# Attention features and experts on one core: projections moved ahead, scatters spread over two tiles, and the norm's root given to ScalarE with one exact step on VectorE

## The chip, the core and the metric

The kernel runs on one core of one Trainium2 chip. The metric is the device time in microseconds of one execution, lower is better. Times shown beside each other come from executions of the same kernel; the traces come from one profiled execution each.

## The reference

Two layers in a row: attention by positive random features, without softmax, and a mixture of eight experts of which each token takes one. Cut to what is computed:

```python
# batch 8, heads 8, seq 576, head_dim 64, 128 features
def phi(x):                       # x = q or k, scaled by 64 ** -0.25
    h = x @ omega.T - sum(x * x) / 2
    return exp(h - max(h)) / sqrt(128)
kv  = einsum('bhsm,bhsd->bhmd', phi(k), v)
z   = phi(k).sum(over s)
att = (phi(q) @ kv) / (phi(q) @ z + 1e-6)
x = att as (4608 tokens, 512)
xn = x / (norm(x) + 1e-6);  en = expert_emb / (norm(expert_emb) + 1e-6)
logits = xn @ en.T / tau
e = argmax(logits);  gate = softmax(logits)[e]
out = gate * (relu(x @ w1[e]) @ w2[e])     # 512 -> 1024 -> 512
```

The queries are drawn larger than the keys. Everything is in float32.

## The kernel before

**Attention** (to about 240 us, its end to 300). 36 tiles of 128 tokens. Iteration `i` of the loop at the end of the first part projects keys of tile `i` and queries of tile `i - 6` (`proj`), each in two halves `a` of four heads, and pairs them: first key half 0 with query half 1, then key half 1 with query half 0. `feats` takes the negative maximum of each head on VectorE (`nm`) and exponentiates on ScalarE (`ft`). `kvmm` adds the keys of tile `i - 1` to the key sums, `qtr` transposes query features (`tr`), `qcopy` copies them out (`qp`), `num` makes the numerators, denominators and logits of a tile (`nu`), and `evacuated` divides them into a row `xr` on VectorE. The order on TensorE and GpSimd, and in the loop on VectorE and ScalarE, is that of the code. Two pairs of PSUM banks, `px` and `py`, hold the projections; the transposes use `px`, the pair of the first projections.

Every third tile, `routed` chooses the expert of three tiles and each token's row in a list sorted by expert, in steps that the lists `spare`, `mid` and `ends` place at points of this and the next iteration; its last step issues three scatters on GpSimd's queue (one per tile) that write the rows `xr` to memory. When the first expert is known, the first two blocks of its tokens are computed between the last attention iterations (`first_steps`).

**Experts** (from about 301 us). 38 steps `t`, each for 128 rows of one expert, the first two within the attention. A step multiplies its rows by `w1` and, two steps behind, hidden rows by `w2`. Each float32 factor is split into a high and a low part, and three products are summed, so a step has 24 + 24 matmuls (`pa` and `nu`). Its other work in the loop, all in the order of the code on every engine:

- VectorE: the low part of the hidden rows (`hl`, L900), the gated result (`scaled`, L247), the high parts of the next weights (`w1h`, `w2h`, L205); then half of the 16-bit planes of the step's products and of the next rows (`pl`, L862), half of the transposed planes put together again (`wd`, L880), and the low part of the rows (`xl`, L899), with which the next step's third matmul begins.
- ScalarE: the other half of the planes (L861) and of the reassembly (L882), the high parts `xh` and `hh` (L894, L896), and the sums of squares of the rows (`sq`, L253).
- GpSimd: the low parts of the weights (`w1l`, `w2l`, L206), and between them the scattered store of a finished block (L272).
- SyncE: transposes of the planes (L868), rows, weights.

The gate needs the norm of each row. It is found for batches of three steps: in steps `t` that 3 divides (and in `SHIFT - 1`), `norms_of` runs on VectorE after the casts and ahead of the first `pl`. It calls `root`, a shift and a subtraction on the bits and three Newton steps, twelve instructions on 128 x 3 numbers (L120 to L131), and two more (L256, L257). `exps_of` then exponentiates the logits with that norm on ScalarE at the end of the step, and in the step after, `inverted` (L265, L266) stands on VectorE at the same place, ahead of `pl`.

Lines of this text are those of the kernel before.

Of the kernel before, what the change touches and what calls it, by code (L numbers as in the profile page):

```python
# [22 lines left out]
P = 128  # L23
# [30 lines left out]
def attention_moe(ctx: ExitStack, tc: tile.TileContext, qT, kT, v1, omT, emb, tau, w1q, w2q, xs, out):  # L54
# [51 lines left out]
    put, got, outs, last_x, junks = [], [], [], [], []  # L106
    W = {"w1": (w1q, w1h, w1l), "w2": (w2q, w2h, w2l)}

    padrow = w1l[:, 1, 2, 0:PAY].bitcast(F32)
    nc.gpsimd.memset(padrow, 0.0)  # L110
    nc.gpsimd.memset(padrow[:, PAY - 1 : PAY], BIGID)
# [135 lines left out]
        nc.vector.tensor_scalar(xg[:, 0:DM], po, gate, None, op0=ALU.mult)  # L247


    def squares(xg, n2):  # L250
        junk = gp.tile([P, DM], BF16, name=f"sq_{len(junks)}", tag="sq", bufs=1)
        junks.append(junk)
        nc.scalar.activation(junk, xg[:, 0:DM], AF.Square, accum_out=n2)  # L253
# [10 lines left out]
    def inverted(total):  # L264
        nc.vector.tensor_scalar(total, total, 1e-9, None, op0=ALU.add)  # L265
        nc.vector.reciprocal(total, total)  # L266
# [13 lines left out]
    with ExitStack() as c1:  # L280
# [104 lines left out]
            )  # L385

        def qtr(i, a):
            st["tr", i, a] = tr = ps.tile([P, 512], F32, name=f"tr{i}_{a}", tag="px", bufs=2)
            for h in range(4):
                nc.tensor.transpose(tr[:, h * P : (h + 1) * P], st["fq", i, a][:, h, :], ident)  # L390

# [21 lines left out]

        def num_out(i):
            g, gi = divmod(i, G)
            st["xr", i] = xr = p1.tile([P, PAY], F32, name=f"xr{i}", tag="xr", bufs=5)
            nc.gpsimd.tensor_copy(xr[:, PAY - 1 :].bitcast(I32), ids[:, i : i + 1])
            if gi == 0:
                st["lg", g] = small.tile([P, G, H, E], F32, name=f"lg{g}", tag="lg", bufs=2)
            rr = small.tile([P, 2, 4], F32, name=f"rr{i}", tag="rr", bufs=3)  # L420
            nc.vector.tensor_scalar(rr, pn[:, :, :, D], EPS, None, op0=ALU.add)
# [14 lines left out]
        def routed(g):  # L436
# [76 lines left out]
        def first_steps():  # L513


            new = lambda n, tag: ps.tile([P, 512], F32, name=f"fs_{n}", tag=tag, bufs=2 if tag == "py" else 1)
# [22 lines left out]
            for t in range(NPRE):  # L539
                hs[t] = rawp.tile([P, F], F32, name=f"hp{t}", tag="raw_w1")  # L540
                turned(xgp[t], 0, new(f"x{t}", f"kv{t}"), *pre_x[t])
                squares(xgp[t], n2[:, t : t + 1])
# [13 lines left out]
            yield from up(1, 1, range(4), new("a11", "py"))  # L556
# [3 lines left out]
            yield from turn(1, 1, "py")  # L560
            yield from down(0, range(4, 8), po)
            yield from down(1, range(8), new("o1", "kv1"))

# [59 lines left out]
        for i in range(NTILE + LAG + 1):  # L623
# [3 lines left out]
            loadq(iq + 2)  # L627
            ks, qs = i < NTILE, 0 <= iq < NTILE
            if ks and qs:
                pairs = [("k", i, 0, "px"), ("q", iq, 1, "px")], [("k", i, 1, "py"), ("q", iq, 0, "py")]  # L630
            elif ks:
                pairs = [("k", i, a, "px") for a in range(2)], []
            else:
                pairs = [("q", iq, a, "py") for a in (1, 0)] if qs else [], []
            filling = i > NTILE
            proj(*pairs[0])
            if later is not None:
                evacuated(later)
            for p in pairs[0][: 1 if i < LAG else 2]:
# [8 lines left out]
            if filling:  # L648
                filled(1 if i <= NTILE + 2 else 2)
            go(spare, i)  # L650
            proj(*pairs[1])
            if later is not None and later % G == G - 1 and later < NTILE - 1:
                steps = routed(later // G)

                for d, key in ((mid, i), (ends, i), (spare, i + 1), (mid, i + 1), (ends, i + 1)):
                    at(d, key).append((next, steps, None))
            go(mid, i)
            if not qs and iq >= 2:
# [213 lines left out]
    with tc.manual_schedule(engines={ET.PE, ET.Activation, ET.DVE, ET.Pool, ET.SP}):  # L872
# [28 lines left out]
            yield  # L901


        n2s, nrms, totals, gates = {}, {}, {}, {}
        batch = lambda t: divmod(t - NPRE, 3)

        def squares_of(*steps):
            for v in steps:
                b, j = batch(v)
                if j == 0:  # L910
                    n2s[b] = few("n2", f"b{b}", 3)
                squares(xg[v], n2s[b][:, j : j + 1])
# [23 lines left out]
        for t in range(NPRE, NSTAT):  # L936
# [36 lines left out]
            computed("w1", t, products(pa[0], xt[t], "w1", par, low, 0, True, True))  # L973
            if t == NPRE or NPRE + 1 < t < XPE - 1:
                xt[t + 1] = x_turned(t + 1, xg[t + 1])
            if t % 3 == 0 and t > SHIFT or t == SHIFT - 1:
                norms_of(batch(t)[0])
            elif t % 3 == 1 and t > SHIFT:
                inverted(totals[batch(t)[0]])
            elif t == SHIFT:  # L980
                inverted(totals[0])
            if near:
                h = words(t)
                nc.scalar.activation(h[:, 0:512], pa[0], AF.Relu)
# [16 lines left out]
            if late and not early:  # L1001
                rejoin(t - 1, wn[0], 0, F, 1)
            if t == SHIFT:
                ended()
            if NPRE + 1 < t < SHIFT:
                split("w2", u)
# [26 lines left out]
            if t % 3 == 0 and t > SHIFT or t == SHIFT - 1:  # L1033
                exps_of(batch(t)[0])
            if t + 3 < NSTAT:
                xg[t + 3] = x_of(t + 3, reg("row", t + 3))
        weights("w2", ends)
        hid[ends] = h_turned(ends, h)
        for u in (ends - 1, ends):
# [10 lines left out]
    with tc.If(tot > NSTAT):  # L1050
        with tc.For_i(NSTAT, tot, 1) as i:
# [9 lines left out]
            squares(xgl, n2)  # L1061
            nrm = root(gp, n2, 1, "x")
            norms(nrm)
            exps(xgl, nrm, total)
# [55 lines left out]
```

## Time and profile before

| | us |
|---|---|
| time, median of 3 runs | 784.7 (780.26 to 785.14) |
| time of the profiled execution | 788.04 |
| its span, first to last instruction | 786.5 |
| attention loop, 35.0 to 240.9 | 205.9 |
| end of attention, tables, 240.9 to 301.3 | 60.4 |
| expert steps 2 to 8, 301.3 to 382.7 | 81.4 |
| expert steps 9 to 36, 382.7 to 743.8 | 361.1 |
| last step and end, 743.8 to 786.5 | 42.7 |

Busy time over the span: TensorE 696.0, VectorE 597.1, ScalarE 382.5, GpSimd 299.1 us. In the profile PE is TensorE's matmuls and PEld its weight loads, DVE is VectorE, ACT ScalarE, POOL GpSimd and SP SyncE. A row of the timeline gives start, duration, engine, line, operation, what is written and read, and in brackets the idle time before it and what ended that. `L120` is a line of the kernel.

The waits and the timeline are read here more than the busy shares: TensorE is busy 88% of the span, and this figure does not tell the rate at which its matmuls run. The clock granted to TensorE is 0.956 on average over the span.

### The profile page before, as it was taken

The numbers are of one execution on the slowest core, as the hardware profiler recorded it, in microseconds if no ns is written. First come the engines' busy times: TensorE is split into PE (matmuls) and PEld (weight loads), VectorE is DVE, ScalarE is ACT, GpSimd is POOL, SyncE is SP. The second block draws the span as 40 slices with busy tenths as digits, with TensorE's granted clock in tenths as the row PEclk, the third lists the DMA queues.
The fourth block names the chain that finished last, engine by engine and source line by source line (L and its number), as shares of the span: only waits on it lengthen the run. The fifth ranks groups of instructions, "written<-read, shape, count | busy, mean of one in ns | idle before, by whom it ended". The sixth has DMA issues, their size and how long they took to land. (4 is left out here: it accounts for less than half of the span.)

```text
span 786.5 us, 17992 instructions
## 1 busy us (share of the span) xinstructions
PE 696.0 (88%) x5977; PEld 570.2 (73%) x5978; DVE 597.1 (76%) x1109; ACT 382.5 (49%) x1038; POOL 299.1 (38%) x296
## 2 busy tenths in 40 slices
PE   6899999998997987998889897989898998989884
PEld 5778878877876775776668685868676776777663
DVE  2368767778876562789798988898889889898951
ACT  4487767767876511732534343434343443434320
POOL 2000111111754232544536363636353544354442
PEclk9999999999999999999999899989999999899988
DMA  5354544548742127845958585867776686858530
GB/s 193 88 157 124 178 156 158 166 150 269 257 166 83 56 78 260 265 125 171 241 132 231 147 215 133 230 149 205 153 211 168 194 196 168 200 163 192 149 94 37
DMA packets 142376, 131.85 MB, mean 168 GB/s; under 512 B 106758, under 2 KB 106886, under 8 KB 142288
## 3 DMA queue, kind: packets, MB, share of 16 engines
q1 hardware_dynamic: 135968, 110.30, 52.1%
q0 software_dynamic: 6320, 20.38, 6.8%
q8 instruction: 55, 0.90, 0.5%
q14 instruction: 33, 0.27, 0.1%
HBM read 83.78 MB, written 21.97 MB: 134 GB/s over the span
## 5 line engine op out<-in xcount | busy, mean ns | idle before, releaser
L206 POOL TENSOR_TENSOR w1l<-raww,w1h 128x1024 f32 x34 | 89.4, 2631 | 218.3 <-DVE w1h L205 213.8
L240 PE MATMUL pa<-w1h,xl 128*128 (+1 forms) x280 | 118.8, 424 | 38.6 <-DVE xl L899 38.6
L240 PE MATMUL nu<-w2h,hh 128*128 (+1 forms) x288 | 113.2, 393 | 6.0 <-DVE xg L247 3.4
L240 PE MATMUL pa<-w1h,xh 128*128 (+1 forms) x280 | 116.5, 416 | 0.5 <-POOL w1l L206 0.2
L240 PE MATMUL pa<-w1l,xh 128*128 (+1 forms) x280 | 115.7, 413 | 0.0
L240 PE MATMUL nu<-w2h,hl 128*128 (+1 forms) x288 | 113.1, 393 | 0.2 <-DVE hl L900 0.2
L240 PE MATMUL nu<-w2l,hh 128*128 (+1 forms) x288 | 112.6, 391 | 0.0
L330 ACT ACTIVATE ftk<-pjk,nmk 128x128 f32<-128x128 f32 x288 | 82.5, 384 | 55.4 <-DVE nmk L327 51.3
L896 ACT ACTIVATE hh<-wd 128x1024 fp32r<-128x1024 f32 x34 | 36.0, 1060 | 130.7 <-DVE wd L880 130.7
L240 PEld LDWEIGHTS pa<-w1h,xl 128*128 128x128 f32 x280 | 56.8, 203 | 58.0 <-DVE xl L899 45.7
L321 PE MATMUL pjk<-om,kt 64*128 64x128 f32 x576 | 88.2, 308 | 9.9 <-DMA kt<-kT 5.3
L330 ACT ACTIVATE ftq<-pjq,nmq 128x128 f32<-128x128 f32 x288 | 84.1, 409 | 13.5 <-DVE nmq L327 13.1
L861 ACT ACTIVATE pl<-pa 128x512 uint16<-128x512 uint16 x68 | 39.5, 586 | 103.3 <-DMA t<-pl 86.5
L206 POOL TENSOR_TENSOR w2l<-raww,w2h 128x1024 f32 x34 | 82.1, 2414 | 8.9 <-DVE w2h L205 8.2
L321 PE MATMUL pjq<-om,qt 64*128 64x128 f32 x576 | 81.2, 294 | 3.2 <-DVE qp L398 1.4
L321 PEld LDWEIGHTS pjk<-om,kt 64*128 64x128 f32 x576 | 71.2, 204 | 16.2 <-issue 7.1
L327 DVE TENSOR_REDUCE nmk<-pjk 128x4 f32<-128x512 f32 x72 | 48.9, 686 | 36.6 <-PE pjk L321 20.0
L321 PEld LDWEIGHTS pjq<-om,qt 64*128 64x128 f32 x576 | 66.8, 194 | 7.7 <-issue 3.8
L472 POOL DMA_INDIRECT xs<-xr,posi x36 | 35.9, 996 | 86.6 <-DVE lg L423 33.7
L240 PEld LDWEIGHTS nu<-w2h,hh 128*128 128x128 f32 x288 | 54.5, 189 | 18.5 <-issue 7.4
L240 PEld LDWEIGHTS pa<-w1h,xh 128*128 128x128 f32 x280 | 57.1, 204 | 13.4 <-POOL w1l L206 0.7
L240 PEld LDWEIGHTS pa<-w1l,xh 128*128 128x128 f32 x280 | 56.6, 202 | 12.8
(297 smaller groups left out, 1363.9 us busy)
## 6 DMA issues: line engine op xcount, KB each, us to landing
raww<-w1q SPq DMA_DIRECT2D x38, 512.0 KB
raww<-w2q SPq DMA_DIRECT2D x38, 512.0 KB
kt<-kT SPq DMA_DIRECT2D x36, 256.0 KB
qt<-qT SPq DMA_DIRECT2D x36, 256.0 KB
xgp<-xs SPq DMA_DIRECT2D x20, 260.5 KB
xg<-xs SPq DMA_DIRECT2D x18, 260.5 KB
rf<-w1q SPq DMA_DIRECT2D x4, 512.0 KB
rf<-w2q SPq DMA_DIRECT2D x4, 512.0 KB
```

Of the source, the lines that this page charges most:

```text
L206: il = nc.gpsimd.tensor_tensor(at(l, dp), raw, at(h, dp).bitcast(F32), op=ALU.subtract)
L240: done.append(nc.tensor.matmul(dst, x[:, c * P : (c + 1) * P], ws.rearrange("p o f -> p (o f)"), start=(begin and i == 0 and k == 0), stop ...
L321: nc.tensor.matmul(st["pj" + w, i, a][:, c, :], st[w, i][r, c, :], om[r, :], start=True, stop=True)
L327: nc.vector.tensor_reduce(nm, pj, axis=AX.X, op=ALU.max, negate=True)
L330: nc.scalar.activation(ft[:, h, :], pj[:, h, :], AF.Exp, bias=nm[:, h : h + 1])
L472: w = nc.gpsimd.indirect_dma_start(out=xs, out_offset=bass.IndirectOffsetOnAxis(ap=posi[:, j : j + 1], axis=0), in_=xr, in_offset=None, bo ...
L861: nc.scalar.activation(planes[1][:, o : o + 512], halved(src)[:, :, 1], AF.Copy)
L896: nc.scalar.activation(hh, wd[:, 0:F], AF.Relu)
```

## The change

Four things change together.

1. **Attention.** Both pairs of projections are issued at the start of an iteration; the key sums, the transposes and the numerators follow. The banks change roles: the first pair and the transposes use `py`, the second pair `px`. Where only keys are projected, iterations alternate between the two pairs of banks; where only queries are, they use `px`. `first_steps` swaps its banks likewise.
2. **Scatters.** `routed` yields before each scatter, so that the three go out at three points of two iterations. There are six buffers `xr` instead of five, and one `lg` instead of two.
3. **The root.** ScalarE takes `Sqrt` of three sums of squares at the start of a step that 3 divides (and of step 4). In the step after, `norms_of` and `exps_of` stand ahead of `scaled`: VectorE forms (n2 / rough + rough) / 2 + 1e-6 and its inverse in five instructions. In the step after that, `inverted` stands at the same place.
4. **Squares.** The unused output of the squares goes to a buffer of the second part, or of the hidden rows in `first_steps`, and not to a pool that lives throughout.

```diff
         def qtr(i, a):
-            st["tr", i, a] = tr = ps.tile([P, 512], F32, name=f"tr{i}_{a}", tag="px", bufs=2)
+            st["tr", i, a] = tr = ps.tile([P, 512], F32, name=f"tr{i}_{a}", tag="py", bufs=2)
...
             for j in range(G):
+                yield
                 xr = st["xr", g * G + j]
                 w = nc.gpsimd.indirect_dma_start(
...
-                pairs = [("k", i, 0, "px"), ("q", iq, 1, "px")], [("k", i, 1, "py"), ("q", iq, 0, "py")]
+                pairs = [("k", i, 0, "py"), ("q", iq, 1, "py")], [("k", i, 1, "px"), ("q", iq, 0, "px")]
             elif ks:
-                pairs = [("k", i, a, "px") for a in range(2)], []
+                pairs = [("k", i, a, ("px", "py")[i % 2]) for a in range(2)], []
             else:
-                pairs = [("q", iq, a, "py") for a in (1, 0)] if qs else [], []
+                pairs = [("q", iq, a, "px") for a in (1, 0)] if qs else [], []
             filling = i > NTILE
             proj(*pairs[0])
+            proj(*pairs[1])
...
             go(spare, i)
-            proj(*pairs[1])
...
+        def roots_of(b):
+            rough[b] = few("rough", f"b{b}", 3)
+            nc.scalar.activation(rough[b], n2s[b], AF.Sqrt, bias=tiny)
 
         def norms_of(b):
-            nrms[b] = root(gp, n2s[b], 3, f"b{b}")
-            norms(nrms[b])
+            nrms[b] = few("nrm", f"b{b}", 3)
+            nc.vector.reciprocal(nrms[b], rough[b])
+            nc.vector.tensor_tensor(nrms[b], nrms[b], n2s[b], op=ALU.mult)
+            nc.vector.tensor_tensor(nrms[b], nrms[b], rough[b], op=ALU.add)
+            nc.vector.tensor_scalar(nrms[b], nrms[b], 0.5, 1e-6, op0=ALU.mult, op1=ALU.add)
+            nc.vector.reciprocal(nrms[b], nrms[b])
...
+            if t == SHIFT - 1 or t > SHIFT and t % 3 == 0:
+                roots_of(batch(t)[0])
+            elif t == SHIFT or t > SHIFT and t % 3 == 1:
+                norms_of(batch(t)[0] if t > SHIFT else 0)
+                exps_of(batch(t)[0] if t > SHIFT else 0)
+            elif t > SHIFT:
+                inverted(totals[batch(t)[0] - 1])
             if t > SHIFT:
                 for v in po:
                     scaled(po[v], xg[v], gates[v])
...
-            if t % 3 == 0 and t > SHIFT or t == SHIFT - 1:
-                norms_of(batch(t)[0])
-            elif t % 3 == 1 and t > SHIFT:
-                inverted(totals[batch(t)[0]])
```

Three places show the moves. In the lists below, a row has the line, the operation, what it writes and reads, and its width; equal neighbours are counted. Numbers in names are those of the tiles.

TensorE in attention iteration 9, before: the end of the first projections, the key sums of tile 8, and the start of the second projections.

```order
L321 MATMUL pjk_0_733<-om,kt_534 128x128
L321 MATMUL pjq_1_734<-om,qt_538 128x128
L345 MATMUL kva_1_0_431<-vt8v,ftk_0_645 64x65 x8
L345 MATMUL kva_1_1_440<-vt8v,ftk_1_697 64x65 x8
L321 MATMUL pjk_1_784<-om,kt_534 128x128
L321 MATMUL pjq_0_785<-om,qt_538 128x128
```

The same place now: from the end of the second projections to the end of the iteration.

```order
L321 MATMUL pjk_1_745<-om,kt_536 128x128
L321 MATMUL pjq_0_746<-om,qt_540 128x128
L345 MATMUL kva_1_0_433<-vt8v,ftk_0_657 64x65 x8
L345 MATMUL kva_1_1_442<-vt8v,ftk_1_699 64x65 x8
L390 MATMUL tr_1_796<-ident,ftq_1_664 128x128 x4
L390 MATMUL tr_0_801<-ident,ftq_0_706 128x128 x4
L409 MATMUL nu<-kvs_0_422,qp_0_711 64x73 x8
```

The second projections have moved ahead of the key sums, and the transposes follow these directly.

VectorE in an expert step of a batch's root, before, from the cast behind `scaled` on (`rtt_b` and `rt_b` are the root's tiles, `n2b` the squares).

```order
L205 COPY w1h<-raww_15_6405 128x1024
L205 ISA
L205 COPY w2h<-raww_13_6407 128x1024
L120 TENSOR_SCALAR rtt_b_6557<-n2b_6269 128x3
L121 TENSOR_SCALAR rt_b_6556<-rtt_b_6557 128x3
L123 TENSOR_TENSOR rtt_b_6557<-n2b_6269,rt_b_6556 128x3
L125 SCALAR_TENSOR_TENSOR rtt_b_6557<-rtt_b_6557,rt_b_6556 128x3
L126 SCALAR_TENSOR_TENSOR rt_b_6556<-rtt_b_6557,rt_b_6556 128x3
```

Now, in the step after `Sqrt`, from `hl` on (`nrmb` is the norm, `roughb` what ScalarE's `Sqrt` gave; the line numbers are the changed kernel's, L249 is `scaled`, L207 the casts, L863 `pl`).

```order
L901 SCALAR_TENSOR_TENSOR hl_6557<-wd_6542,hh_6556 128x1024
L922 RECIPROCAL nrmb_6593<-roughb_6500 128x3
L923 TENSOR_TENSOR nrmb_6593<-nrmb_6593,n2b_6231 128x3
L924 TENSOR_TENSOR nrmb_6593<-nrmb_6593,roughb_6500 128x3
L925 TENSOR_SCALAR nrmb_6593<-nrmb_6593 128x3
L926 RECIPROCAL nrmb_6593<-nrmb_6593 128x3
L249 TENSOR_SCALAR xgp_105<-nu,totalb_6245 128x512
L147 TENSOR_LOAD tabi
L207 ISA
L207 COPY w1h<-raww_16_6496 128x1024
```

The work on the norm has moved from behind the casts to ahead of `scaled`, and from fourteen instructions to five.

ScalarE around the end of a batch, before: squares, the three exponentials of a batch, planes.

```order
L253 ACTIVATE sq_7619,n2b_7618<-xgp_106 128x512
L262 ACTIVATE ex_7622,totalb_7621<-xg_5050,rt_b_7543 128x8
L262 ACTIVATE ex_7624,totalb_7621<-xgp_104,rt_b_7543 128x8
L262 ACTIVATE ex_7626,totalb_7621<-xgp_105,rt_b_7543 128x8
L861 ACTIVATE pl_1_7642<-pa_0_7643 128x512
L861 ACTIVATE pl_1_7642<-xg_5048 128x512
```

Now: one batch's `Sqrt` with its table load at the start of a step, and the next step's load for the exponentials.

```order
L253 ACTIVATE sq_7168,n2b_6972<-xg_5049 128x512
L917 ACT_TABLE_LOAD
L917 ACTIVATE roughb_7175<-n2b_6972,tiny 128x3
L862 ACTIVATE pl_1_7186<-pa_0_7187 128x512
L862 ACTIVATE pl_1_7186<-xg_5050 128x512
L883 ACTIVATE wd_7217<-t_20_0_7131 128x512
L883 ACTIVATE wd_7217<-t_20_1_7133 128x512
L862 ACTIVATE pl_1_7186<-pa_1_7188 128x512
L895 ACTIVATE xh_7228<-wd_7217 128x512
L897 ACTIVATE hh_7231<-wd_7217 128x1024
L253 ACTIVATE sq_7261,n2b_7260<-xg_5050 128x512
L262 ACT_TABLE_LOAD
```

`Sqrt` and a load have come in ahead of the planes of one step, and the exponentials, with a load ahead of them, have moved from the end of that step to behind the next squares.

More of the change, by code (lines that the diff above doesn't have):

```diff
@@ L107, in attention_moe @@
     W = {"w1": (w1q, w1h, w1l), "w2": (w2q, w2h, w2l)}
+    tiny = const.tile([P, 1], F32, name="tiny")
+    nc.vector.memset(tiny, 1e-37)
     padrow = w1l[:, 1, 2, 0:PAY].bitcast(F32)
@@ L247, in scaled, with squares @@
         nc.vector.tensor_scalar(xg[:, 0:DM], po, gate, None, op0=ALU.mult)
-    def squares(xg, n2):
-        junk = gp.tile([P, DM], BF16, name=f"sq_{len(junks)}", tag="sq", bufs=1)
-        junks.append(junk)
+    def squares(xg, n2, junk):
         nc.scalar.activation(junk, xg[:, 0:DM], AF.Square, accum_out=n2)
@@ L415, in num_out @@
             g, gi = divmod(i, G)
-            st["xr", i] = xr = p1.tile([P, PAY], F32, name=f"xr{i}", tag="xr", bufs=5)
+            st["xr", i] = xr = p1.tile([P, PAY], F32, name=f"xr{i}", tag="xr", bufs=6)
             nc.gpsimd.tensor_copy(xr[:, PAY - 1 :].bitcast(I32), ids[:, i : i + 1])
             if gi == 0:
-                st["lg", g] = small.tile([P, G, H, E], F32, name=f"lg{g}", tag="lg", bufs=2)
+                st["lg", g] = small.tile([P, G, H, E], F32, name=f"lg{g}", tag="lg", bufs=1)
             rr = small.tile([P, 2, 4], F32, name=f"rr{i}", tag="rr", bufs=3)
@@ L513, in first_steps @@
         def first_steps():
-            new = lambda n, tag: ps.tile([P, 512], F32, name=f"fs_{n}", tag=tag, bufs=2 if tag == "py" else 1)
+            new = lambda n, tag: ps.tile([P, 512], F32, name=f"fs_{n}", tag=tag, bufs=2 if tag == "px" else 1)
             hs = {}
@@ L541, in first_steps @@
                 turned(xgp[t], 0, new(f"x{t}", f"kv{t}"), *pre_x[t])
-                squares(xgp[t], n2[:, t : t + 1])
+                squares(xgp[t], n2[:, t : t + 1], hs[t][:, 0:DM])
                 yield
@@ L555, in first_steps @@
             inverted(total)
-            yield from up(1, 1, range(4), new("a11", "py"))
+            yield from up(1, 1, range(4), new("a11", "px"))
             po = new("o0", "kv0")
@@ L559, in first_steps @@
             yield from turn(1, 0, "kv1")
-            yield from turn(1, 1, "py")
+            yield from turn(1, 1, "px")
             yield from down(0, range(4, 8), po)
@@ L650, in attention_moe @@
             go(spare, i)
-            proj(*pairs[1])
             if later is not None and later % G == G - 1 and later < NTILE - 1:
                 steps = routed(later // G)
-                for d, key in ((mid, i), (ends, i), (spare, i + 1), (mid, i + 1), (ends, i + 1)):
+                for d, key in ((mid, i), (ends, i), (spare, i + 1), (mid, i + 1), (ends, i + 1), (ends, i + 1), (ends if i + 2 > NTILE + LAG else mid, min(i + 2, NTILE + LAG)), (ends, min(i + 2, NTILE + LAG))):
                     at(d, key).append((next, steps, None))
@@ L901, in summed @@
             yield
-        n2s, nrms, totals, gates = {}, {}, {}, {}
+        n2s, rough, nrms, totals, gates = {}, {}, {}, {}, {}
         batch = lambda t: divmod(t - NPRE, 3)
@@ L911, in squares_of @@
                     n2s[b] = few("n2", f"b{b}", 3)
-                squares(xg[v], n2s[b][:, j : j + 1])
+                squares(xg[v], n2s[b][:, j : j + 1], p2.tile([P, DM], BF16, name=f"sq{v}", tag="sq", bufs=1))
+        def roots_of(b):
+            rough[b] = few("rough", f"b{b}", 3)
+            nc.scalar.activation(rough[b], n2s[b], AF.Sqrt, bias=tiny)
         def norms_of(b):
-            nrms[b] = root(gp, n2s[b], 3, f"b{b}")
-            norms(nrms[b])
+            nrms[b] = few("nrm", f"b{b}", 3)
[4 more added lines that the diff above has]
+            nc.vector.reciprocal(nrms[b], nrms[b])
         def exps_of(b):
@@ L1003, in attention_moe @@
             if t == SHIFT:
+                inverted(totals[0])
                 ended()
@@ L1032, in attention_moe @@
                 squares_of(t + 2)
-            if t % 3 == 0 and t > SHIFT or t == SHIFT - 1:
-                exps_of(batch(t)[0])
             if t + 3 < NSTAT:
@@ L1038, in attention_moe @@
         hid[ends] = h_turned(ends, h)
+        inverted(totals[batch(ends)[0]])
         for u in (ends - 1, ends):
@@ L1060, in attention_moe @@
             n2, total = few("n2", "x", 3)[:, 0:1], few("total", "x", 3)[:, 0:1]
-            squares(xgl, n2)
+            squares(xgl, n2, p2.tile([P, DM], BF16, name="sqx", tag="sq", bufs=1))
             nrm = root(gp, n2, 1, "x")
```

2 lines of the change are left out of this document (removed).

## The prediction

> **What bounds the kernel now.** I read the page's 40 slices first: TensorE is busy nearly everywhere, so the question is where it waits or runs slowly. From the start of expert step 9 to that of step 37 the windows view and the list of waits say this (columns: stretch, its length, busy time of PE, PEld, DVE, ACT, POOL with instruction counts, clock, DMA share, GB/s; then engine, line, waited for, total, times, longest).
>
> ```profile
> 382.70:743.80 361.10, 325.84 (x1344) 262.77 (x1345) 317.83 (x431) 151.95 (x305) 169.75 (x85) 0.95 0.72 183
> ...
> PE pa L240 <- DVE xl L899: 35.2, 16, 3.7
> ACT pl L861 <- DMA t<-pl: 76.2, 23, 4.6
> ```
>
> TensorE's only large wait here is on VectorE's `xl`, 35.2 us. The TensorE timeline shows how it falls. The rows with `pa<-w1h,xh` at 0.39 are the starts of steps 26 to 29, the other two lie in step 28:
>
> ```profile
> 605.09 0.39 PE L240 MATMUL pa<-w1h,xh 128*128 x1
> ...
> 615.97 0.39 PE L240 MATMUL pa<-w1h,xh 128*128 x1
> ...
> 626.85 0.39 PE L240 MATMUL pa<-w1h,xh 128*128 x1
> ...
> 630.69 0.50 PE L240 MATMUL pa<-w1h,xl 128*128 x1 [3.23 <-DVE xl L899]
> ...
> 633.05 0.63 PE L240 MATMUL pa<-w1h,xl 128*128 x1
> ...
> 642.86 0.39 PE L240 MATMUL pa<-w1h,xh 128*128 x1
> ```
>
> Steps 26 and 27 take 10.88 us with no wait. Step 28 takes 16.01: 3.23 idle, and afterwards matmuls of 0.63 instead of 0.39. The 28 steps of the stretch last 361.1 us; at 10.88 they would last 304.6. The surplus is 56.5 us: 35.2 waiting and some 21 at the slower rate that follows. Why `xl` is late every third step stands in the timelines of VectorE and GpSimd for the step before:
>
> ```profile
> 616.34 1.23 DVE L900 SCALAR_TENSOR_TENSOR hl<-wd,hh 128x1024 fp32r<-128x1024 f32 x1 [0.57 <-ACT hh L896]
> ...
> 618.14 0.68 DVE L205 CAST w1h<-raww 128x1024 f32 x1
> ...
> 619.34 2.37 DVE L120 TENSOR_SCALAR rtt_b<-n2b 128x3 int32<-128x3 int32 x1
> ...
> 622.15 3.15 DVE L125 SCALAR_TENSOR_TENSOR rtt_b<-rtt_b,rt_b 128x3 f32<-128x3 f32 x1
> 625.33 0.16 DVE L126 SCALAR_TENSOR_TENSOR rt_b<-rtt_b,rt_b 128x3 f32<-128x3 f32 x1
> 625.53 0.16 DVE L123 TENSOR_TENSOR rtt_b<-n2b,rt_b 128x3 f32<-128x3 f32 x1
> ...
> 627.20 0.68 DVE L862 COPY pl<-pa 128x512 uint16<-128x512 uint16 x1
> ...
> 608.36 2.62 POOL L206 TENSOR_TENSOR w1l<-raww,w1h 128x1024 f32 x1 [6.04 <-DVE w1h L205]
> ...
> 612.16 2.42 POOL L206 TENSOR_TENSOR w2l<-raww,w2h 128x1024 f32 x1
> ...
> 619.06 2.63 POOL L206 TENSOR_TENSOR w1l<-raww,w1h 128x1024 f32 x1 [4.48 <-PE pa L240]
> ...
> 622.86 2.41 POOL L206 TENSOR_TENSOR w2l<-raww,w2h 128x1024 f32 x1
> ```
>
> The root of three numbers keeps VectorE from 619.34 to 627.20. Most of that isn't work: a 0.16 us instruction took 3.15 and ended as GpSimd's `w2l` ended (625.27), and L120 ended with `w1l`. So VectorE stands behind GpSimd's two subtractions, and `pl<-pa`, which was ready at 620.12 (ScalarE's `pl` below), starts 7 us late. Everything to `xl` follows it.
>
> **The change, part by part.**
>
> *The root.* Per batch 14 small VectorE instructions go and five come, now between `hl` and L247. There GpSimd is idle: `w2l` ended at 614.58, and the next `w1l` starts only after the cast that stands behind them. So they cost about 0.20 each start to start (625.33 to 625.53), 1.0 us together. Upper end: one of them meets a GpSimd instruction, 3.2 as L125; lower end: hidden in a VectorE pause, 0. I take 1.0, since the rows beside that place show no pause but the 0.57. The `total` pair (L265, L266) moves to the same place in the step after. It took
>
> ```profile
> L265 DVE TENSOR_SCALAR totalb<-totalb 128x3 f32<-128x3 f32 x12 | 24.8, 2067 | 0.0
> ```
>
> 2.07 for the same reason, and will take 2 x 0.20 = 0.4. Behind these in VectorE's queue stand L247, the casts and so GpSimd: all shift by that much.
>
> *What is late next.* Not TensorE's own 10.88 alone. `w1l` to `w1l` is 619.06 - 608.36 = 10.70 in a step without a root, and that is a loop of its own: `w1l`, the store and `w2l` take 6.2, the second `wd` copy waits for `w2l`'s end, then `xl`, `hl`, L247 and the cast release the next `w1l`. The new instructions lie on this loop: three steps are 3 x 10.70 + 1.0 + 0.4 = 33.5, against 32.6 for TensorE. So 11.17 per step, with TensorE waits of some 0.3, too short for the slow matmuls (they stood after 3.23 idle, and not in the 12.24 us step below with its wait of 1.05). For 28 steps 312.7.
>
> *Steps that lock.* Where `pl<-pa` comes late after the start of `w1l`, the copy behind it meets GpSimd's next work:
>
> ```profile
> 572.10 0.69 DVE L862 COPY pl<-pa 128x512 uint16<-128x512 uint16 x1 [2.72 <-issue]
> 572.71 2.82 DVE L862 COPY pl<-xgp 128x512 uint16<-128x512 uint16 x1
> ...
> 569.01 2.62 POOL L206 TENSOR_TENSOR w1l<-raww,w1h 128x1024 f32 x1 [6.02 <-DVE w1h L205]
> ...
> 565.78 0.50 PE L240 MATMUL pa<-w1h,xl 128*128 x1 [1.05 <-DVE xl L899]
> ...
> 578.02 0.50 PE L240 MATMUL pa<-w1h,xl 128*128 x1 [1.06 <-DVE xl L899]
> ...
> L862 DVE COPY pl<-xgp 128x512 uint16<-128x512 uint16 x14 | 24.0, 1716 | 0.0
> L862 DVE COPY pl<-xg 128x512 uint16<-128x512 uint16 x13 | 20.0, 1542 | 0.3 <-DMA xg<-xs 0.3
> ```
>
> Here it comes 3.09 us after it, and `w1l` is already over: the copy takes 2.82, the planes go late to the transposes, these let `pl<-pa` go late again, and the step is 12.24 (565.78 to 578.02). The two group rows, of the same 28 steps, say how often: a free copy takes about 0.5, a held one 2.9, and a mean of 1.6 makes 12 of 27 held. The nine `total` pairs of the stretch, right ahead of `pl<-pa` today, explain most; they move away. The new instructions also push `w1l` back against `pl<-pa`, which makes it rarer in two of three steps. I allow three such steps: 3 x (12.24 - 11.17) = 3.2, and 0.5 for recovery, together 316.4. Saved between steps 9 and 37: 361.1 - 316.4 = 44.7.
>
> *ScalarE.* Twelve `Sqrt` of 3 columns and 24 table loads come, since `Sqrt` and `Exp` alternate; a load's one row and the gap into which they fall are
>
> ```profile
> L330 ACT ACT_TABLE_LOAD x1 | 1.3, 1283 | 1.0 <-PEq L1107 1.0
> ...
> 616.21 0.61 ACT L253 ACTIVATE sq<-xg 128x512 bf16<-128x512 f32 x1
> ...
> 619.52 0.60 ACT L861 ACTIVATE pl<-pa 128x512 uint16<-128x512 uint16 x1 [2.60 <-DMA t<-pl]
> ...
> 631.68 0.29 ACT L262 ACTIVATE ex<-xgp,rt_b 128x8 f32<-128x8 f32 x1
> 631.87 0.19 ACT L262 ACTIVATION_READ_ACCUMULATOR ex<-xgp,rt_b 128x1 f32 x1
> ```
>
> `sq` ends at 616.91 with its accumulator, `pl` begins at 619.52 when the transposes let go. Load and `Sqrt` take 1.28 + 0.29 = 1.57 of these 2.6: hidden. In the next step the load runs while `Exp` waits for VectorE's norms (`hl` + 1.0, here 618.6), and three exponentials, whose rows start 0.28 apart with their accumulators between, 0.9 in all, bring ScalarE to 619.5: `pl` just in time. I take 0; ends: 0 (nothing is removed from ScalarE, so no gain) and 12 x (2 x 1.28 + 0.29) = 34 if no pause covers them. If that cover went, `pl<-pa` and the planes cycle would be late by it. The Trainium skill speaks against this step: "ScalarE: Activation LUTs", section "What ACT_TABLE_LOAD costs", gives about 2.66 us for a switch with its drain, and its section "Table sets: the hidden batching unit" asks to finish the calls of one set before those of another. By an estimate from that page the batch pays 5.6 us on ScalarE instead of 2.9; in the `Sqrt` step some 0.35 us would stick out of the 2.6, which makes 12 x 0.35 = 4 us more, 735. No run here shows a drain beside a load.
>
> *Step 37 and steps 7, 8.* Step 37 has the same wait:
>
> ```profile
> 747.77 0.80 PE L240 MATMUL pa<-w1h,xl 128*128 x1 [3.35 <-DVE xl L899]
> ...
> 364.56 0.47 PE L240 MATMUL nu<-w2h,hh 128*128 x1 [1.61 <-ACT xh L227]
> ...
> 376.81 0.47 PE L240 MATMUL nu<-w2h,hh 128*128 x1 [1.12 <-DVE xg L247]
> ```
>
> By step 28 the slow matmuls after it add 16.01 - 10.88 - 3.23 = 1.9, so it is worth 3.35 + 1.9 = 5.2. The 1.61 and 1.12 of steps 7 and 8 follow the root of step 6: 2.7.
>
> *Attention, projections first.* The loop there closes like this (VectorE and TensorE; the last row is the list of waits from 5 to 36 us):
>
> ```profile
> 51.77 0.17 DVE L421 TENSOR_SCALAR rr<-nu 128x8 f32<-128x8 f32 x1 [0.50 <-PE nu L409]
> ...
> 55.95 0.33 PE L390 MATMUL tr<-ident,ftq 128*128 128x128 f32 x1 [0.38 <-ACT ftq L330]
> ...
> 57.83 0.17 DVE L421 TENSOR_SCALAR rr<-nu 128x8 f32<-128x8 f32 x1 [0.16 <-PE nu L409]
> ...
> PE pjk L321 <- ACT ftk L330: 1.1, 3, 0.5
> ```
>
> Numerators end, VectorE evacuates them and takes the maxima, ScalarE exponentiates the first pair, TensorE transposes and does the next numerators: 57.83 - 51.77 = 6.06 us. Moving the second projections ahead of the key sums changes nothing on that way; TensorE stands at the transposes for `ftq` before and after, only VectorE's second maxima come earlier. I take 0. The nearest row for both ends is this 0.38: over the 30 iterations in which keys and queries run together (6 to 35), -11 if the wait vanishes and +11 if the second projections wait as long for an exponential that still reads their bank, with key sums, transposes and numerators queued behind them. In the first six iterations alternating banks save the waits on `ftk`, 1.1; ends 0 and the same again. The scatters stay 36 on GpSimd, three of a group apart instead of in a row; nothing in the loop above waits for them, so 0, and by the same 0.38 for twelve groups -5 to +5.
>
> **Sum.** 44.7 + 5.2 + 2.7 + 1.1 = 53.7. The profiled execution took 788.0 (span 786.5), so 734.3; the median of the runs, 784.7, lies 3.3 lower: 731.
>
> **The rivals.**
> *TensorE alone bounds.* If VectorE's pause absorbs the new instructions, every step is 10.88: 304.6, and 56.5 + 5.2 + 2.7 + 1.1 = 65.5 are saved: 719. For it: steps 26 and 27 ran so; against: 10.70 leaves only 0.18 to absorb 0.47.
> *The transposes take the root's place.* If most steps lock at 12.24, 28 of them are 342.7: 18.4 + 5.2 + 2.7 + 1.1 = 27.4 saved: 757. For it: 12 of 27 copies were held; against: the pair that held most of them moves, and `w1l` is pushed back.
> *Slower: table switches on the path.* If a load doesn't run in ScalarE's pause but holds the plane copies, each batch pays. It decides at (53.7 + 8) / 12 = 5.1 us exposed per batch. Two loads that each also empty ScalarE, at twice the row, with `Sqrt` and exponentials (5.1 + 0.3 + 0.9 = 6.3) make 76 us: 807. Against: the pauses before `pl`, 2.6 here, 76.2 over 23 cases and 4.6 at most. The Trainium skill's page on ScalarE (section "What ACT_TABLE_LOAD costs") has a switch at about twice the row.
> *It does nothing.* If `xl` were late for another reason than the root, 782; the VectorE rows leave little room.
>
> **How the numbers follow.** Chances: my sum 0.50 (own range 724 to 740), TensorE alone 0.22, locked steps 0.20, no gain 0.04, slower 0.03, and 0.01 between. The range 714 to 754 leaves out the worse part of the locked case, the last two and a little at the bottom, together 0.2. A measurement of this kernel can tell about 1% from no change; by that faster 0.93, same 0.04, slower 0.03.
>
> **What would show it.** Right: no TensorE wait over 2 us on `xl` between steps 9 and 37, no 0.63 us matmuls there, norms of 0.2 each before L247's successor, step periods of 10.9 to 11.3, ScalarE's table loads inside its pause, attention periods of 6.06. Wrong: 12.24 periods in most steps, loads that end after `pl` could start, a longer attention loop.

## The result and the profile after

| | before | after |
|---|---|---|
| median of four runs each (us) | 784.5 (780.3 to 785.1) | 724.5 (723.7 to 724.9) |
| ratio, 95% interval | | 0.9245 (0.9212 to 0.9279) |
| profiled execution, its span (us) | 788.0, 786.5 | 724.5, 722.9 |
| start to expert step 2 | 301.3 | 294.7 |
| step 2 to step 9 | 81.5 | 76.8 |
| step 9 to step 37 | 361.1 | 314.5 |
| step 37 to the end | 42.7 | 36.9 |

The predicted 731 lies 6.5 us above. The gain of 63.6 us in the span is 6.5 + 4.7 + 46.6 + 5.8. The bounds of the stages are starts in TensorE's timeline; the first row is of before, the other three are of after (start, length, engine, line, operation).

```profile
301.27 0.50 PE L240 MATMUL pa<-w1h 128*128 128x512 f32 x1 [0.69 <-ACT w1h L227]
```

```profile
294.73 0.50 PE L242 MATMUL pa<-w1h 128*128 128x512 f32 x1 [0.69 <-ACT w1h L229]
...
371.52 0.39 PE L242 MATMUL pa<-w1h,xh 128*128 x1
...
685.97 0.39 PE L242 MATMUL pa<-w1h,xh 128*128 x1
```

The windows view of after between steps 9 and 37, in the columns of the prediction's first fence:

```profile
371.50:686.00 314.50, 313.67 (x1346) 251.91 (x1345) 293.11 (x344) 181.41 (x335) 169.59 (x84) 1.00 0.80 209
```

And its list of waits there (engine, line, waited for: total, times, longest):

```profile
POOL w1l L208 <- DVE w1h L207: 138.9, 28, 6.0
...
PE pa L242 <- DVE xl L900: 0.8, 2, 0.5
```

TensorE's 35.2 us of waiting on `xl` are 0.8 now, and it is busy for 313.7 of 314.5 us. The steps are alike: 11.15 to 11.22 us nearly all, two of 11.8 and 11.9, and none of 12.24 or 16. VectorE's timeline of after shows what has become of the root:

```profile
518.47 1.23 DVE L901 SCALAR_TENSOR_TENSOR hl<-wd,hh 128x1024 fp32r<-128x1024 f32 x1 [0.56 <-ACT hh L897]
519.61 0.17 DVE L922 RECIPROCAL nrmb<-roughb 128x3 f32<-128x3 f32 x1
519.82 0.16 DVE L923 TENSOR_TENSOR nrmb<-nrmb,n2b 128x3 f32<-128x3 f32 x1
...
520.41 0.18 DVE L926 RECIPROCAL nrmb<-nrmb 128x3 f32<-128x3 f32 x1
520.50 0.74 DVE L249 TENSOR_SCALAR xgp<-nu,totalb 128x512 f32<-128x512 f32 x1
...
522.36 0.68 DVE L863 COPY pl<-pa 128x512 uint16<-128x512 uint16 x1
```

From the start of the first of the five to that of the scaling are 0.89 us, where the fourteen took 7.86 before (619.34 to 627.20); the first of the pair that inverts the totals has a group row of 2,067 ns in before and this in after:

```profile
L265 DVE TENSOR_SCALAR totalb<-totalb 128x3 f32<-128x3 f32 x12 | 1.9, 162 | 0.0
```

GpSimd's timeline of after gives the loop of three steps:

```profile
510.73 2.40 POOL L208 TENSOR_TENSOR w1l<-raww,w1h 128x1024 f32 x1 [4.76 <-DVE w1h L207]
...
522.08 2.64 POOL L208 TENSOR_TENSOR w1l<-raww,w1h 128x1024 f32 x1 [5.36 <-DVE w1h L207]
...
533.27 2.63 POOL L208 TENSOR_TENSOR w1l<-raww,w1h 128x1024 f32 x1 [4.95 <-DVE w1h L207]
```

With the step ahead of these (11.00, from 499.73) they make 33.5 us, which the prediction had. But it also expected TensorE to finish each step in 10.88 and then to wait some 0.3. It doesn't wait. Two starts of after that are one step apart say why:

```profile
506.87 0.40 PE L242 MATMUL pa<-w1h,xh 128*128 x1
...
518.04 0.39 PE L242 MATMUL pa<-w1h,xh 128*128 x1
```

48 matmuls without a pause take 11.17 us, 0.2327 each; before they took 10.88, 0.2267 each. TensorE has become 2.6% slower, in a change that doesn't touch its instructions here. The granted clock doesn't tell the two apart: it is 1.00 in the row of after above, and it was 1.00 in steps 26 and 27 of before. Which of the two, VectorE's and GpSimd's loop or TensorE, then sets the 11.16, the trace can't tell, since both need the same time.

### The profile page after: what moved, and what is told of

It reads as the page before. It is cut to its first block, busy times and chain, and to the rows that moved or that the text cites. A ratio compares the mean times of both kernels' runs of the same rounds, so it can differ in the third digit from the quotient of the medians.

```text
span 722.9 us, 17880 instructions
## 1 busy us (share of the span) xinstructions
PE 671.5 (93%) x5977; PEld 553.4 (77%) x5978; DVE 562.9 (78%) x1002; ACT 418.8 (58%) x1074; POOL 301.6 (42%) x296
## 5 line engine op out<-in xcount | busy, mean ns | idle before, releaser
L881 DVE COPY wd<-t 128x1024 uint16<-128x1024 uint16 x68 | 116.1, 1710 | 1.1 <-DMA t<-pl 1.0
L242 PE MATMUL pa<-w1h,xl 128*128 (+1 forms) x280 | 110.9, 396 | 0.8 <-DVE xl L900 0.8
L242 PE MATMUL pa<-w1h,xh 128*128 (+1 forms) x280 | 111.0, 396 | 0.0
L242 PE MATMUL pa<-w1l,xh 128*128 (+1 forms) x280 | 110.5, 395 | 0.0
L321 PE MATMUL pjk<-om,kt 64*128 64x128 f32 x576 | 76.9, 291 | 6.8 <-DMA kt<-kT 5.4
L321 PE MATMUL pjq<-om,qt 64*128 64x128 f32 x576 | 73.6, 287 | 3.2 <-ACT ftq L330 1.4
L321 PEld LDWEIGHTS pjk<-om,kt 64*128 64x128 f32 x576 | 65.9, 195 | 9.8 <-issue 5.5
L242 PEld LDWEIGHTS pa<-w1h,xl 128*128 128x128 f32 x280 | 52.6, 188 | 15.4 <-DVE xl L900 2.9
L242 PEld LDWEIGHTS nu<-w2h,hl 128*128 128x128 f32 x288 | 54.2, 188 | 13.0 <-DVE hl L901 0.3
L242 PEld LDWEIGHTS nu<-w2l,hh 128*128 128x128 f32 x288 | 54.2, 188 | 12.8
```

What stands on the lines that cost most here:

```text
L242: done.append(nc.tensor.matmul(dst, x[:, c * P : (c + 1) * P], ws.rearrange("p o f -> p (o f)"), start=(begin and i == 0 and k == 0), stop ...
L321: nc.tensor.matmul(st["pj" + w, i, a][:, c, :], st[w, i][r, c, :], om[r, :], start=True, stop=True)
L881: nc.vector.tensor_copy(to, src)
```

## The experiments

Kernels of one set ran on one chip, and each time is compared with before on that chip (771.5 us for the first set, 788.0 for the second, 785.5 for the third). The ratio is the comparison's, with its 95% interval; the step is the mean from step 9 to step 37 in the profiled execution, and the spacing is the median from one expert matmul's start to the next, pauses left out. Read so, before has 12.90 and 0.227, and after 11.23 and 0.232.

| kernel | us | ratio | step | spacing |
|---|---|---|---|---|
| e_align | 717.0 | 0.9268 (0.9229 to 0.9308) | 11.22 | 0.232 |
| e_shift | 772.0 | 0.9997 (0.9973 to 1.0022) | 12.86 | 0.227 |
| e_root | 715.0 | 0.9274 (0.9230 to 0.9318) | 11.24 | 0.232 |
| e_attn | 770.3 | 0.9978 (0.9948 to 1.0009) | 12.86 | 0.227 |
| e_addr | 725.5 | 0.9200 (0.9173 to 0.9227) | 11.23 | 0.227 |
| e_addr_before | 782.0 | 0.9914 (0.9883 to 0.9945) | 12.83 | 0.232 |
| e_nonorm | 723.8 | 0.9180 (0.9141 to 0.9219) | 11.16 | 0.232 |
| e_nonorm_addr | 717.3 | 0.9109 (0.9080 to 0.9139) | 11.03 | 0.227 |
| e_newton | 742.4 | 0.9464 (0.9405 to 0.9523) | 11.83 | 0.227 |
| e_oldplace | 750.2 | 0.9536 (0.9480 to 0.9591) | 12.03 | 0.232 |
| e_scat | 727.9 | 0.9279 (0.9221 to 0.9337) | 11.23 | 0.232 |
| e_best | 716.8 | 0.9112 (0.9049 to 0.9174) | 10.90 | 0.227 |

### TensorE's rate, first try: 32 bytes

The new constant `tiny` takes 32 bytes ahead of the weight buffers, which so no longer start at a multiple of 64. e_align gives it a width that restores this; e_shift adds `tiny` to before.

```diff
-    tiny = const.tile([P, 1], F32, name="tiny")
+    tiny = const.tile([P, 16], F32, name="tiny")[:, 0:1]
```

> After, with 16 columns instead of one in the small constant `tiny`, so that the four weight buffers and what lies behind them start at multiples of 64 bytes again, as before the change (the one column moved them by 32 bytes). In the changed kernel the experts' matmuls start 0.232 us apart, before 0.227. Theory A (the 32 bytes slow TensorE, but VectorE's and GpSimd's loop of 33.46 us per three steps sets the pace anyway): spacing back to 0.227, steps still 11.15 on average, now with TensorE waits on `xl` of about 0.27 a step, total 721 to 725. Theory B (TensorE's slower rate sets the pace): spacing 0.227 and steps of 10.88 to 11.0, total about 716. Theory C (the rate has another cause, such as the load without pauses): spacing stays 0.232, 724.5.

> Before, with nothing but the constant `tiny` of one column added (set once, never read), so that the weight buffers start 32 bytes later. If the place of the tiles sets TensorE's rate: matmul spacing 0.232 instead of 0.227, steps without a wait 11.15 instead of 10.88, some of it taken from the waits on `xl`; total 785 to 791. If the rate comes from something else: spacing 0.227, total 784.5.

Neither spacing moved: 0.232 stays in e_align (its theory C), and 0.227 in e_shift (its second case). Multiples of 64 have nothing to do with it.

### The two parts alone

e_root has the root's part of the diff on top of before, e_attn all the rest.

> Before, with the root's part of the change alone (Sqrt on ScalarE, five VectorE instructions and the inversion of the totals ahead of the scaling; the one-column constant too). By the prediction's terms 784.5 - 44.7 - 5.2 - 2.7 = 732; by what the trace of the changed kernel shows from expert step 2 on (46.6 + 5.8 + 4.7) 727. If the root's part needs the attention part to work, 750 or more.

> Before, with everything of the change except the root's part (projections first, alternating banks, scatters apart). By the prediction 784.5 - 1.1 = 783.4. By the trace of the changed kernel, whose first expert steps begin 6.5 us earlier, 778, with TensorE's full clock from about 11 us instead of 20 and no gain in the attention iterations that follow. If that gain is another run's chance, 784.

The root's part alone gives 0.9274 and the attention part 0.9978, an interval that holds 1; their product is 0.925. So the gain is the root's part's. The slower spacing came with the root's part, though TensorE's program in it is that of e_shift but for the counts it waits for. What does differ is where the tiles lie: the new small tiles `rough` and `nrm` take 128 bytes ahead of the expert steps' tiles. In the programs as built, counted modulo 256 bytes, operands and hidden tiles (stationary in these matmuls) start at the same place as the weight buffers (moving) in the three kernels with 0.227 and 128 bytes off in the three with 0.232.

### TensorE's rate, second try: 128 bytes, and which of the two sets the pace

e_addr changes only that place in after, and e_addr_before only that place in before. e_nonorm shortens VectorE's loop, and e_nonorm_addr does both.

```diff
 e_addr:
-            rough[b] = few("rough", f"b{b}", 3)
+            rough[b] = few("rough", f"b{b}", 19)[:, 0:3]
 e_addr_before:
+    spare = gp.tile([P, 32], F32, name="spare", bufs=1)
+    nc.vector.memset(spare, 0.0)
 e_nonorm:
-            nc.vector.reciprocal(nrms[b], rough[b])
-            nc.vector.tensor_tensor(nrms[b], nrms[b], n2s[b], op=ALU.mult)
-            nc.vector.tensor_tensor(nrms[b], nrms[b], rough[b], op=ALU.add)
-            nc.vector.tensor_scalar(nrms[b], nrms[b], 0.5, 1e-6, op0=ALU.mult, op1=ALU.add)
+            nc.vector.tensor_scalar(nrms[b], rough[b], 1e-6, None, op0=ALU.add)
             nc.vector.reciprocal(nrms[b], nrms[b])
```

> After, with ScalarE's rough roots stored in tiles of 19 columns instead of 3, so that the operands and hidden tiles of the expert steps lie 128 bytes further on and, counted modulo 256 bytes, at the same place as the weight buffers again. In the six kernels traced so far the experts' matmuls start 0.227 us apart where the two agree modulo 256 (before, the constant alone, the attention part alone) and 0.232 where they are 128 apart (after, its 64-byte constant, the root's part alone). If that place sets TensorE's rate: spacing 0.227. Then theory A (VectorE's and GpSimd's loop of 33.46 us per three steps sets the pace): steps still 11.15 on average and TensorE waits on `xl` of about 0.27 a step, 0.924 of before; theory B (TensorE's rate sets the pace): steps of 10.88 to 10.95, 0.914 of before. If the rate belongs to the root's part and not to the place: 0.232 and 11.16.

> Before, with a spare tile of 128 bytes ahead of the expert steps' tiles, so that these lie 128 bytes off the weight buffers modulo 256 bytes. If the place sets TensorE's rate: spacing 0.232 to 0.2335, steps without a wait 11.15 instead of 10.88, of which the waits on `xl` give back a part: 0 to 6 us slower. If not: 0.227 and no difference.

> After, with the exact step of the root left out: two VectorE instructions per batch (add 1e-6, invert) instead of five, so the gates rest on ScalarE's rough root alone. VectorE's loop then needs 33.46 - 0.6 = 32.86 per three steps, 10.95 each. Theory A (the loop sets the pace): 11.05 or less per step where TensorE lets it, so limited by TensorE's own 11.15 (spacing 0.232): no gain. Theory B: none either, 11.16.

> Both edits together: two VectorE instructions instead of five, and the tiles 128 bytes further on. If the place sets TensorE's rate and the loop sets the pace: steps of 10.95 (the loop), 28 x 0.2 = 5.7 us less than with either edit alone, 0.916 of before. If the loop doesn't bind: 10.88 as with the place alone. If the place doesn't matter: 11.16.

The place sets the rate, in both directions: e_addr has 0.227 and e_addr_before 0.232. Two starts of e_addr_before that are one step without a wait apart, 11.15 us where before has 10.88:

```profile
539.11 0.40 PE L242 MATMUL pa<-w1h,xh 128*128 x1
...
550.26 0.39 PE L242 MATMUL pa<-w1h,xh 128*128 x1
```

The edits move all tiles of the expert steps together, so they don't tell which of these tiles counts. In e_addr the faster rate changes nothing of the mean step. Its windows, list of waits and TensorE timeline:

```profile
370.50:684.90 314.40, 310.35 (x1345) 250.76 (x1345) 291.69 (x344) 178.83 (x335) 169.85 (x85) 1.00 0.81 210
```

```profile
PEld pa L242 <- DVE xl L900: 11.8, 19, 1.6
```

```profile
506.15 0.39 PE L242 MATMUL pa<-w1h,xh 128*128 x1
506.38 0.39 PE L242 MATMUL pa<-w1l,xh 128*128 x1
506.72 0.50 PE L242 MATMUL pa<-w1h,xl 128*128 x1
```

The stretch is 314.4 us as in after. The faster TensorE now stands at the first matmul with `xl`: it starts 0.34 after its neighbour instead of 0.23, the weight load having waited, and its steps mostly read 10.88, 11.39, 11.17. That is the picture of the prediction, with 33.44 for three steps. With the slow spacing a shorter loop brings little (e_nonorm, 11.16, TensorE's own 48 x 0.2325, against 11.23 in after, whose two longer steps are gone); with both edits the step falls to 11.03, where 10.95 was expected. So loop and TensorE stand side by side at 11.16 in the changed kernel, and neither yields alone. The fourth corner, after itself, ran on another chip, so this rests on the steps in the traces and on the two single edits' ratios, 0.9200 and 0.9180 against 0.9109 for both. e_addr_before is a miss: TensorE is slower in it by 2.6%, and the kernel is not slower but 0.9% faster. Its trace shows only that the loop gives the loss back: from step 9 to step 37 TensorE's waits on `xl` are 29.1 us for 35.2 in the trace of before (another chip), and the stretch is 359.1 for 361.1. Why it comes out faster stays open.

### Place or number, and the scatters

e_newton puts the old root of 14 instructions at the new place; e_oldplace puts the five new ones behind the casts; e_scat issues a group's three scatters in a row again.

```diff
 e_newton, in norms_of (and no Sqrt):
+            nrms[b] = root(gp, n2s[b], 3, f"b{b}")
+            norms(nrms[b])
 e_oldplace:
-            elif t == SHIFT or t > SHIFT and t % 3 == 1:
+            elif t == SHIFT:
...
+            if t % 3 == 1 and t > SHIFT:
+                norms_of(batch(t)[0])
             if near:
...
+            if t % 3 == 1 and t > SHIFT:
+                exps_of(batch(t)[0])
             if t + 3 < NSTAT:
 e_scat, and without the three points for them:
             for j in range(G):
-                yield
...
```

> After, with the old root on VectorE (14 instructions and the pair that inverts, no Sqrt on ScalarE) at the new place, between `hl` and the scaling. If it is the place that freed the loop, none of the small instructions is held by GpSimd there: 16 x 0.2 = 3.2 us per batch instead of 1.0, so 33.46 + 2.2 = 35.7 per three steps, 11.9 each, about 20 us more than after in steps 9 to 37 (0.95 of before). If the count of instructions was the cost, holds of 2.4 and 3.15 us appear here too and three steps take 38 or more (0.98 of before).

> After, with the five short root instructions back at the old place, behind the casts and ahead of `pl<-pa`, and the exponentials back at the end of the step. If GpSimd's subtractions hold small VectorE instructions there, the first takes until the end of `w1l` (about 2.4 us) or one of them until the end of `w2l` (3 us), `pl<-pa` of these steps goes 3 us late, and a part comes back as steps of 12.2 or more: 11.4 to 12.3 per step on average (0.935 to 0.965 of before). If only the number of instructions matters: 11.16 as after.

> After, with the scatters of a group of three tiles in a row again, as before the change, but the projections still first. By the prediction (scatters cost nothing on the loop): no difference to after. If the spread scatters are what lengthens the iterations from 6.06 to 6.46 and 7.16 in the traces of the kernels with the attention part: the expert steps begin 4 to 8 us earlier.

In e_newton no small instruction is held. VectorE's timeline, first and last of the 14 and the scaling behind them, then the windows row:

```profile
524.31 0.16 DVE L122 TENSOR_SCALAR rtt_b<-n2b 128x3 int32<-128x3 int32 x1
...
526.89 0.18 DVE L257 RECIPROCAL rt_b<-rt_b 128x3 f32<-128x3 f32 x1
526.98 0.74 DVE L249 TENSOR_SCALAR xgp<-nu,totalb 128x512 f32<-128x512 f32 x1
```

```profile
367.90:699.00 331.10, 314.41 (x1346) 254.25 (x1345) 298.00 (x425) 152.45 (x306) 170.69 (x85) 0.98 0.77 200
```

They take 2.67 us instead of 7.86 at the old place, and the step 11.83 (11.9 expected). Of the 46.6 us between steps 9 and 37, 361.1 - 331.1 = 30.0 come with the new places of root, exponentials and inversion, since the attention part alone leaves the step at 12.86 (e_attn, as e_shift). The other 16.6 come with the shorter root; e_addr, which has e_newton's spacing, gives 331.1 - 314.4 = 16.7. e_oldplace, VectorE and then GpSimd:

```profile
499.25 0.17 DVE L922 RECIPROCAL nrmb<-roughb 128x3 f32<-128x3 f32 x1
499.45 2.17 DVE L923 TENSOR_TENSOR nrmb<-nrmb,n2b 128x3 f32<-128x3 f32 x1
501.66 0.16 DVE L924 TENSOR_TENSOR nrmb<-nrmb,roughb 128x3 f32<-128x3 f32 x1
```

```profile
498.96 2.63 POOL L208 TENSOR_TENSOR w1l<-raww,w1h 128x1024 f32 x1 [4.47 <-PE pa L242]
```

L923 has three columns and takes 2.17 us, until `w1l` ends at 501.59. L922, which also runs within `w1l`, isn't held, and the other three start when `w1l` is over. The Trainium skill, "SBUF — State Buffer", section "Who interferes with whom", lets a VectorE instruction with two inputs in that memory contend with a GpSimd instruction that reads it, and one with a single input only in a two-port mode, which copies, casts and tensor-scalar instructions can enter. The rows agree: L923 has two such inputs, L922, a reciprocal, one. And L120 and L265, held for 2.37 and 2.07 us in before, are tensor-scalar instructions with one input, so a single input doesn't save an instruction by itself. The step is 12.03, but not all of it is the hold. The totals' first instruction waits for the exponentials, which this kernel put at the step's end:

```profile
L265 DVE TENSOR_SCALAR totalb<-totalb 128x3 f32<-128x3 f32 x9 | 1.5, 169 | 14.9 <-ACT ex L262 14.9
```

That is up to 14.9 of the 22.2 us more than in after (336.7 against 314.5). So this run shows the hold, but doesn't give its price alone. In e_scat the expert steps begin at 294.2 us and last 11.23, as in after (294.7 and 11.23, on another chip): no cost of the scatters shows, in either order.

### Both bounds moved

e_best keeps the exact step and gives three of its instructions, and one of the totals', to GpSimd; its tiles lie as in e_addr.

```diff
+        def halves_of(b):
+            nrms[b] = few("nrm", f"b{b}", 3)
+            nc.vector.reciprocal(nrms[b], rough[b])
+            nc.gpsimd.tensor_tensor(nrms[b], nrms[b], n2s[b], op=ALU.mult)
+            nc.gpsimd.tensor_tensor(nrms[b], nrms[b], rough[b], op=ALU.add)
+            nc.gpsimd.tensor_scalar(nrms[b], nrms[b], 0.5, 1e-6, op0=ALU.mult, op1=ALU.add)
...
+            if t == SHIFT - 1 or t > SHIFT and t % 3 == 0:
+                halves_of(batch(t)[0])
             if late and not early:
                 sm = summed(t - 1, *wn)
```

> After, with the tiles 128 bytes further on as in the second set, and VectorE's share of the small work cut from seven instructions per batch to three: the product, sum and scaling of the exact step and the addition to the totals go to GpSimd, which waits 5 us per step there. VectorE's loop is then 3 x 10.70 + 3 x 0.2 = 32.7 per three steps, 10.90 each, about TensorE's own 10.88: 28 x (11.16 - 10.90) = 7.3 us less than after in steps 9 to 37, 0.91 of before. If GpSimd's small instructions delay `w1l` or hold VectorE's copies: 11.2 or more, no gain.

Its windows row and list of waits:

```profile
373.70:678.90 305.20, 304.87 (x1345) 252.15 (x1344) 277.93 (x309) 181.87 (x335) 184.83 (x122) 1.00 0.84 216
```

```profile
POOL w1l L208 <- DVE w1h L207: 72.4, 20, 4.5
...
POOL w1l L208 <- PE pa L242: 32.7, 8, 4.5
ACT pl L862 <- PE pa L242: 28.7, 32, 2.7
```

The first of these 28 steps takes 11.50 and all others 10.88, and GpSimd and ScalarE now wait for TensorE: it alone is the bound. 716.8 us stand beside 727.9 for e_scat on the same chip, 1.5% less, and 0.9112 of before against 0.9279 for e_scat and 0.9245 for the change.

## Why the prediction was right, and where not

*The bound.* Right. The root stood behind GpSimd's two subtractions, and `xl` behind the root. e_newton and e_oldplace show both halves: at the new place even 14 instructions run free; at the old one, of only five, one is held (L923, 2.17 us in the mean of nine).

*The root and the totals.* 1.0 and 0.4 us were summed; 0.89 is measured for the five, the pair's first instruction takes 0.16 instead of 2.07, and e_addr's three steps make 33.44 for 33.5.

*What is late next.* Half right, and the step that failed: "against 32.6 for TensorE ... with TensorE waits of some 0.3". The loop was right and binds (e_addr). TensorE's 10.88 was carried over from before, although the change adds tiles ahead of others, and their place sets its rate: three steps of TensorE are 33.5, too. This hid behind the loop and cost nothing, so the forecast of 11.17 holds although one of its two durations was wrong, and that is luck. But it takes away most of what a shorter loop would have won: with loop and place both changed, e_best takes 9.3 us less between steps 9 and 37, and e_nonorm, with the loop alone, 2.0. The rival "TensorE alone bounds" named an engine that does bind, beside the loop, with the wrong duration.

*Steps that lock.* Mis-sized: 3.2 and 0.5 were allowed for three steps of 12.24, and none came. In after all the plane copies are held, as their group rows say (means, in ns):

```profile
L863 DVE COPY pl<-xg 128x512 uint16<-128x512 uint16 x15 | 28.9, 1928 | 0.9 <-DMA xg<-xs 0.9
...
L863 DVE COPY pl<-xgp 128x512 uint16<-128x512 uint16 x14 | 27.7, 1978 | 0.6 <-DMA xgp<-xs 0.6
```

But they are held by `w1l`, which starts 0.28 ahead of `pl<-pa` in nearly every step (522.08 and 522.36 above), and not by what comes after it. Being held doesn't matter by itself, only until when. Of the 3.7 us allowed on top of 312.7 only 1.8 came, most of it in the two steps of 11.8 and 11.9. This is why the stretch gave 46.6 and not 44.7.

*ScalarE.* Right at 0, in these rows of after:

```profile
508.11 0.19 ACT L253 ACTIVATION_READ_ACCUMULATOR sq<-xg 128x1 f32 x1
508.31 1.28 ACT L917 ACT_TABLE_LOAD   x1
509.61 0.30 ACT L917 ACTIVATE roughb<-n2b,tiny 128x3 f32<-128x3 f32 x1
509.87 0.60 ACT L862 ACTIVATE pl<-pa 128x512 uint16<-128x512 uint16 x1
...
519.07 1.28 ACT L262 ACT_TABLE_LOAD   x1
520.62 0.30 ACT L262 ACTIVATE ex<-xgp,nrmb 128x8 f32<-128x8 f32 x1 [0.27 <-DVE nrmb L926]
...
521.49 0.58 ACT L862 ACTIVATE pl<-pa 128x512 uint16<-128x512 uint16 x1
```

The load starts as the squares end and `Sqrt` as the load ends, 1.30 later. The second load even runs in a wait, for VectorE's norms. ScalarE's `pl` now starts straight behind `Sqrt` or the exponentials, so its pause there is used up. But its half still ends ahead of VectorE's, by 0.7 us at the least (here it begins at 521.49, VectorE's at 522.36), so no pair of planes is complete later for the loads. The Trainium skill, "ScalarE: Activation LUTs", section "What ACT_TABLE_LOAD costs", adds a drain that about doubles the load; here the 1.28 agrees, and no drain shows on either side of it.

*Steps 2 to 8 and step 37.* 2.7 and 5.2 were summed, 4.7 and 5.8 came. The first is the root's part's as well (77.7 in e_root against 83.3 in e_shift). Of its 2.0 more, 1.0 is a wait of TensorE on VectorE's `pl` (L226) in before, which wasn't counted and is gone in after.

*Attention.* The largest miss: 1.1 + 0 was summed, and the expert steps begin 6.5 us earlier. The views of one tile (`rr`, count, lengths, first and last start) and of groups before 30 us, of before and of after:

```profile
L421 DVE TENSOR_SCALAR rr<-nu x36: 151/165/168, 51.8 to 286.7; 128x8 f32<-128x8 f32 x36
...
L321 PE MATMUL pjk<-om,kt 64*128 64x128 f32 x96 | 13.9, 393 | 8.8 <-DMA kt<-kT 5.3 <-DVE rowc L92 1.9 <-ACT ftk L330 1.1
```

```profile
L421 DVE TENSOR_SCALAR rr<-nu x36: 151/165/168, 44.3 to 280.2; 128x8 f32<-128x8 f32 x36
...
L321 PE MATMUL pjk<-om,kt 64*128 64x128 f32 x120 | 12.7, 324 | 5.5 <-DMA kt<-kT 5.4 <-DVE enbd L601 0.2
```

The iterations from the first `rr` to the last are the same within 1.0 us (234.9 and 235.9), as predicted; the gain is 7.5 us ahead of them. With fewer waits at the start the slow matmuls also end sooner, 324 ns in the mean for 393. The prediction had priced this for step 28, and here it counted the waits alone. Little of it can be relied on: on the first set's chip e_attn begins its iterations 3.7 us earlier than e_shift (45.9 against 49.6), needs 7.8 more for them, so that its expert steps begin 3.7 later (287.9 against 284.2), and its time can't be told from before's. What lengthens the iterations there stays open.

*The sum.* In the profiled execution 53.7 were summed and 63.5 came: 5.4 more in attention, 2.0 in steps 2 to 8, 1.9 in steps 9 to 36, 0.6 at the end. The medians, 784.5 and 724.5, are 60.0 apart, since the profile of before lay 3.6 above its median and that of after on it.

## What to carry to other kernels

A tiny instruction on VectorE costs what stands in front of it: look where GpSimd is idle before shortening the work, then do both. When two engines need the same time per step, an edit to either shows nothing; a two by two of edits finds that out. And after an edit that adds or moves a tile, read the spacing of matmuls again before carrying over a rate.

## What the runs showed of the hardware

The experts' matmuls (512 columns, 4 bytes each) start 0.227 us apart where the stationary operand's tile and the moving operand's buffer agree modulo 256 bytes, and 0.232 where they are 128 apart: so in all fourteen kernels, seven of each, whatever else they do. Offsets of 32 or 64 bytes common to both change nothing. But in the programs as built the tiles start at 128 or 160 modulo 256 in the seven fast kernels and at 0, 32 or 64 in the seven slow ones. So the runs don't tell whether the distance from the weight buffers counts or the tiles' own place. Other distances, and the mechanism, stay open.

An instruction of three columns can be held until a GpSimd subtraction ends (2.17 us for L923 in e_oldplace, 3.15 for L125 in before), and 14 such instructions need 2.67 us together where GpSimd is idle (e_newton). A table load of ScalarE takes 1.28 us (mean of 24 in after); it follows the squares without a pause, and `Sqrt` follows it without one (508.30 to 508.31, 509.59 to 509.61).

The same kernel of before has medians of 771.5, 785.5 and 788.0 us on three chips.
